# Bank and order changes in a fused attention-and-MLP kernel: two transposing tiles get other PSUM banks, and the instruction lists are reordered

## The chip, the cores and the metric

The kernel runs on one core of a Trainium2 chip. The metric is the device time of one execution in microseconds (us), lower is better. TensorE (PE) multiplies matrices into PSUM, VectorE (DVE), ScalarE (ACT) and GpSimd (POOL) work on tiles, and SyncE (SP) mainly issues transfers (DMAs). The engines run side by side; each takes its own list of instructions in order and waits for the others through semaphores.

## The reference

The output mixes two branches of the same rows x (2048 x 512, bf16) by a gate. Cut to what matters:

```python
x = A_x
g = _sigmoid((x * gate_w).sum(-1, keepdims=True))
# branch a: linear attention, 32 heads of width 16
q, k, v = (x @ wqkv) split into heads
pq, pk = q @ w_phi, k @ w_phi                      # per head
phi = concat(softmax(p), softmax(-p))              # for pq and pk
kv, z = phi_k.T @ v, phi_k.sum(rows)               # per head
o = (phi_q @ kv) / (phi_q @ z + 1e-6)
a = o @ wo
# branch b: MLP
b = relu(x @ w1) @ w2                              # w1: 512 x 1376
return g * a + (1 - g) * b
```

## The kernel before

The rows are 16 tiles of 128, in four chunks of four. Every step of the work is a task with a name; for each engine one list in ORDER (L17 to L63) says in which order its tasks stand, and `emit` (L127) writes them out, with a semaphore wait wherever a task depends on another engine or on a DMA. Nothing is reordered later: what stands first in a list blocks what stands behind it.

Tasks that the prediction speaks of, m a tile, c a chunk, J a job (k0 to k8, q0 to q8, one or two tiles each):

- **Loads** (SP, L276 to L292): xa and xb are the first three tiles of x and the fourth, wva and wvb the halves of the value weights, w1a, w1b and w1c parts of w1; wkT is a transposing load of the key weights, and x1, x2, x3 are transposing loads of the later chunks of x.
- **First chunk of x**: xt{m}a and xt{m}b (L321) turn tile m on TensorE by products with the identity, into two PSUM banks that XB (L317) names; xe{m}0 on ScalarE (L333) and xe{m}1 on VectorE (L335) move them to XT in SBUF. A tile may only be turned once the bank has been emptied of the tile that used it.
- **Values**: v{m} (L369) multiplies a tile with the value weights, for the first four tiles in halves v{m}a and v{m}b, which need wva and wvb; banks 2, 3, 4, 5. ve{m} (ScalarE, L374) moves the result to SBUF.
- **MLP, first half**: h{c}_{k} (L392) and its relu rl{c}_{k} (ScalarE, L410); hr{c} is the remainder with the gate's column (L400), rr{c}, gr{c}, ge{c}, gp{c}, go{c} make the gate's factors, and ht{c} (SP, L421) turns the remainder. Banks 3, 4, 5.
- **Folds**: f1_{j}, f0_{j} (L351) multiply wk or wq with w_phi; fe.. moves them out.
- **Feature jobs**: pr_J (L449) is the projection, ev_J its eviction (ScalarE, L482), mx_J and mn_J maximum and minimum per head (VectorE, L486, L488), t1_J and t2_J the two subtractions (GpSimd, L495), ex_J the exponential (ScalarE, L500), sm_J the sums, rc_J the reciprocals (VectorE), nm_J the scaling (GpSimd, L509 for k, L532 for q); q jobs have ra_J (GpSimd, L528) ahead of nm_J.
- **Key summary**: kv{m} (L516) adds up over all tiles in banks 6 and 7; kn and kz (VectorE, L547, L549) copy it out.
- **Query stage**: tq{m} (SP, L535) turns a tile of query features by DMA, nd{m}_{half} (L559) makes numerators and denominators, rd and o (VectorE, L565, L567) divide, to{m} (SP, L572) turns the result, b{m} (L580) is the second MLP product and a{m} (L586) adds the attention's output product into the same bank, oe{m} (ScalarE, L631) evicts and st{m} stores. b{m} needs the bank that oe{m-3} has emptied. The last tile's b15 and a15 are split in columns (L601, L612), with one part evicted by VectorE (L622).

TensorE's list begins with warm0, a block of idle products (L251), then xt0a to xt2b, the value and MLP products of the first chunk, and the folds. The other engines' lists follow that order of need.

Of the kernel before, what the change touches and what calls it, by code (L numbers as in the profile page):

```python
# [15 lines left out]

ORDER = {  # L17
    "sp": (
        "xa wva xb wvb w1a wphi wkT w1b x1 gw w1c wqT x2 x3 w2a ht0 w2b ht1 wo ht3 tq0 tq1 tq3 tq2 to0 to1 tq4 "
        "tq5 to2 to3 tq6 tq7 to4 ht2 to5 tq9 tq8 to6 to7 tq10 tq11 to8 to9 tq12 tq13 to10 to11 tq14 tq15 to12 "  # L20
        "to13 to14 to15 st15_1 "
    ),
    "pool": (
# [5 lines left out]
    ),  # L29
    "act": (  # L30
# [8 lines left out]
    ),  # L39
    "dve": (  # L40
# [10 lines left out]
    ),  # L51
# [10 lines left out]
    ),  # L62
}  # L63

# [16 lines left out]
class _Graph:  # L81
# [6 lines left out]
    def add(self, name, eng, fn, deps=(), dur=0.1, lat=None, dma=False):  # L88
        assert name not in self.tasks, name
        found = []  # L90
        for d in deps:
            if d is None:
                continue
            t = self.tasks[d]
            if t not in found:
                found.append(t)
        self.tasks[name] = _Task(name, eng, fn, found, dur, self.LAT[eng] if lat is None else lat, dma)
        return name
# [44 lines left out]
def bass_gated_mix__linear_kernel_hedgehog__dense_activation_relu__prompt_kernel(  # L143
# [11 lines left out]
    x2 = A_x.rearrange("b s d -> (b s) d")  # L155
# [25 lines left out]
    with ExitStack() as es:  # L181
# [54 lines left out]
        add = g.add  # L236
# [71 lines left out]
        wbd = [f"wbd{j}" for j in range(ND)]  # L308


        def evict(name, eng, out_, b, deps):
            if eng == "act":
                add(name, eng, lambda q: q.activation(out_, PS[:, b, :], ACT.Copy), deps, dur=0.6)
            else:
                add(name, eng, lambda q: q.tensor_copy(out_, PS[:, b, :]), deps, dur=0.69)

        XB, FB = ((0, 1), (6, 7), (0, 1), (6, 7)), (6, 7, 0, 1)  # L317

        def pe_xt(q, m, n):
            for j in (2 * n, 2 * n + 1):  # L320
                last = q.matmul(PS[:, XB[m][n], (j % 2) * P:(j % 2 + 1) * P], XN[:, m, j * P:(j + 1) * P],  # L321
                                IDN[:, :], start=True, stop=True)
            return last

        for m in range(4):
            for n in range(2):
                add(f"xt{m}{'ab'[n]}", "pe", lambda q, m=m, n=n: pe_xt(q, m, n),
                    ("xa" if m < 3 else "xb", "ident", f"xe{m - 2}{n}" if m > 1 else None), dur=0.11)
            for n, eng in enumerate(("act", "dve")):
                xo = XT[:, 2 * n:2 * n + 2, m * P:(m + 1) * P]  # L330
                xi = PS[:, XB[m][n], 0:2 * P].rearrange("p (j t) -> p j t", j=2)
                if eng == "act":
                    add(f"xe{m}{n}", eng, lambda q, o=xo, i=xi: q.activation(o, i, ACT.Copy), (f"xt{m}a",), dur=0.38)  # L333
                else:
                    add(f"xe{m}{n}", eng, lambda q, o=xo, i=xi: q.tensor_copy(o, i), (f"xt{m}b",), dur=0.42)  # L335
# [13 lines left out]
        def pe_fold(q, s, j, b):  # L349
            for i in range(ND):  # L350
                last = q.matmul(PS[:, b, i * P:(i + 1) * P], WT[:, s * ND + i, j * P:(j + 1) * P], WBD[:, i, :],  # L351
                                start=True, stop=True)
            return last

        for j in range(ND):
            b = FB[j]
            add(f"f1_{j}", "pe", lambda q, j=j, b=b: pe_fold(q, 1, j, b), ("wkT", *wbd, f"xe{3 - j // 2}{j % 2}"), dur=0.24)
            evict(f"fe1_{j}", ("dve", "act")[j % 2], WP[:, 1, j, :], b, (f"f1_{j}",))
        units = []
        for c in range(NC):  # L360
# [6 lines left out]
        def pe_v(q, m, js, b):  # L367
            for j in js:
                last = q.matmul(PS[:, b, :], XT[:, j, m * P:(m + 1) * P], WV[:, j, :],  # L369
                                start=(j == 0), stop=(j == ND - 1))  # L370
            return last

        def evict_v(m, b, deps):
            add(f"ve{m}", "act", lambda q: q.activation(  # L374
                ap(VS, NT * NG * GZ, m * NG * GZ, [[GZ, NG], [1, GV]]), psap(b * 512, [[GV, NG], [1, GV]]), ACT.Copy),
                deps, dur=0.6)

        for m in range(4):
            for n, js in enumerate(((0, 1), (2, 3))):
                add(f"v{m}{'ab'[n]}", "pe", lambda q, m=m, js=js: pe_v(q, m, js, VB[m]),  # L380
                    (f"xe{m}{n}", f"wv{'ab'[n]}", *((f"v{m}a",) if n else ())), dur=0.44)
            evict_v(m, VB[m], (f"v{m}b",))
        freed = {b: (f"ve{m}",) for m, b in enumerate(VB)}
        add("gt", "pe", lambda q: q.matmul(PS[:, 2, 0:ND], GWR[:, :], IDN[:, 0:ND], start=True, stop=True),
# [19 lines left out]
        n = 0  # L404
        for kind, a, k in units:
            b = HB[n % len(HB)]
# [23 lines left out]
        for c in range(NC):  # L430
# [3 lines left out]
                dur=0.2)  # L434
# [3 lines left out]
        for m in range(4, NT):  # L438
            add(f"v{m}", "pe", lambda q, m=m: pe_v(q, m, range(ND), 2), (*xof[m // 4], "wva", "wvb", f"ve{m - 1}" if m > 4 else "gv"),
                dur=0.865)  # L440
# [15 lines left out]
        for jn, (kind, tiles) in enumerate(jobs):  # L456
            w = len(tiles)
            n = kind_n[kind]
# [32 lines left out]
            for tn, M, sg in (("t1", MX, 0), ("t2", MN, 1)):  # L491
                o3 = ap(TS, NTS * 2 * F, ts * 2 * F + sg * GV, [[2 * GV, w * NG], [DH, GH], [1, DH]])
                m3 = ap(M, NSL * 2 * H, sl * 2 * H, [[GH, w * NG], [1, GH], [0, DH]])
                a3, b3 = (pb3, m3) if sg == 0 else (m3, pb3)
# [27 lines left out]
            else:  # L522
# [4 lines left out]
                    dur=0.11 + 0.207 * w)  # L527
# [24 lines left out]
                for m in tiles:  # L552
# [22 lines left out]
                    ab = HB[m % 3]  # L575
# [15 lines left out]
                    if m == NT - 1:  # L591
# [15 lines left out]
                        for h2 in range(2):  # L607
                            b, cs = hb[h2], cols[h2]
# [12 lines left out]
                            else:  # L621
                                add(f"oe{m}_1", "dve", lambda q, m=m, b=b, cs=cs: q.tensor_scalar(  # L622
                                    OSB[:, m % NOS, cs], PS[:, b, 0:cs.stop - cs.start], OMG[:, m:m + 1], None, ALU.mult), need,
                                    dur=0.4)
# [57 lines left out]
```

## Time and profile before

| | |
|---|---|
| median of 3 runs | 150.82 us (150.82 to 150.91) |
| profiled execution | 150.61 us |
| its span in the trace | 148.8 us |
| TensorE busy | 145.4 us, 98% |
| VectorE, GpSimd, ScalarE busy | 110.9, 109.7, 91.8 us |
| chain that ended last, by engine | POOL 46%, PE 42%, issue 5%, DMA 3% |
| TensorE clock granted | full in all 40 slices |

The profile is one execution, taken by the hardware profiler; its time is a little below the median of the runs. Busy time of TensorE is a sum of overlapping bars: a product's bar lasts 379 ns where the next starts 216 ns after it, so pauses are found from starts, not from bars. The chain of waits goes back from the last instruction to whatever released it, again and again. Landing times of DMAs are counted from the start of their issue.

### The profile page before, as it was taken

How to read it: one execution, taken by the hardware profiler on the slowest of the kernel's cores; microseconds unless marked ns; L12 is line 12 of the kernel's file. 1: busy time of each engine (PE TensorE's matmuls, PEld its weight loads, DVE VectorE, ACT ScalarE, POOL GpSimd, SP SyncE). 2: the span in 40 equal slices, each digit the busy share in tenths (PEclk: the TensorE clock that was granted, in tenths of full speed). 3: DMA queues.
4: the chain of work that ended last, by engine and by line, in shares of the span. 5: the costliest groups of instructions: out<-in, count | busy, mean ns of one | idle time of the engine just before them, and what ended most of it. 6: DMA issues, size and time to landing. Idle time of an engine off the chain costs nothing.

```text
span 148.8 us, 2554 instructions
## 1 busy us (share of the span) xinstructions
PE 145.4 (98%) x984; PEld 73.1 (49%) x984; DVE 110.9 (75%) x169; ACT 91.8 (62%) x127; POOL 109.7 (74%) x73
## 2 busy tenths in 40 slices
PE   7999999999999999999999999999999999999994
PEld 2454444445446644455455544454545445445453
DVE  0345799999997769893979979799899966618301
ACT  3367779996795987865988691656545651303051
POOL 4000899999999999999999999999999924510000
PEclk9999999999999999999999999999999999999999
DMA  4999999300200500000000135964737587874543
GB/s 164 289 224 185 261 206 289 109 0 0 66 0 0 154 31 0 0 0 0 4 2 0 35 87 127 108 152 95 181 71 176 151 206 142 162 160 116 127 141 110
DMA packets 45524, 16.11 MB, mean 108 GB/s; under 512 B 39272, under 2 KB 45384, under 8 KB 45512
## 3 DMA queue, kind: packets, MB, share of 16 engines
q1 hardware_dynamic: 43208, 13.89, 42.9%
q10 hardware_dynamic: 2304, 2.06, 4.3%
q8 instruction: 8, 0.13, 0.4%
q14 instruction: 4, 0.03, 0.1%
HBM read 4.41 MB, written 2.10 MB: 44 GB/s over the span
## 4 chain that ended last, share of the span: by engine, by line
POOL 46%; PE 42%; issue 5%; DMA 3%; DVE 1%; SPq 1%; ACT 1%
POOL TS L495 25%; PE PS L580 19%; POOL FT L509 18%; PE PS L586 9%; DMA PHQ<-FT 3%; POOL FT L532 3%; PE PS L559 3%; PE PS L369 2%; PE PS L251 2%; PE PS L449 2%; PE PS L392 2%; PE PS L601 2%; SPq L535 1%; PE PS L321 1%; PE PS L351 1%
## 5 line engine op out<-in xcount | busy, mean ns | idle before, releaser
L495 POOL TENSOR_TENSOR TS<-MN,PB 128x1024 bf16<-128x1024 bf16 (+1 forms) x18 | 31.0, 1733 | 12.9 <-DVE MN L488 12.9
L392 PE MATMUL PS<-XT,W 128*128 128x512 bf16 x160 | 38.4, 379 | 0.0
L502 DVE TENSOR_REDUCE ZB<-FT 128x128 f32<-128x2048 bf16 (+1 forms) x18 | 36.4, 2029 | 1.9 <-ACT FT L500 1.8
L580 PE MATMUL PS<-W,HT 128*128 128x512 bf16 (+1 forms) x165 | 37.8, 379 | 0.0
L500 ACT ACTIVATE FT<-TS 128x2048 bf16<-128x2048 bf16 (+1 forms) x18 | 30.9, 1719 | 4.3 <-POOL TS L495 3.6
L495 POOL TENSOR_TENSOR TS<-PB,MX 128x1024 bf16<-128x1024 bf16 (+1 forms) x18 | 31.1, 1732 | 0.0
L449 PE MATMUL PS<-WP,XT 128*128 128x512 bf16 x128 | 30.1, 379 | 0.0
L509 POOL TENSOR_TENSOR FT<-FT,SC 128x2048 bf16<-128x2048 bf16 (+1 forms) x9 | 29.7, 3308 | 0.0
L631 ACT ACTIVATE OSB<-PS,OMG 128x512 bf16<-128x512 f32 x15 | 10.3, 686 | 24.9 <-PE PS L586 24.8
L410 ACT ACTIVATE HT<-PS 128x512 bf16<-128x512 f32 x40 | 22.6, 596 | 4.7 <-PE PS L392 3.9
L580 PEld LDWEIGHTS PS<-W,HT 128*128 128x128 bf16 (+1 forms) x165 | 15.4, 98 | 17.2 <-ACT OSB L631 0.7
L482 ACT ACTIVATE PB<-PS 128x1024 bf16<-128x1024 f32 (+1 forms) x18 | 16.7, 928 | 10.7 <-PE PS L449 5.7
L392 PEld LDWEIGHTS PS<-XT,W 128*128 128x128 bf16 x160 | 14.7, 98 | 16.4 <-ACT HT L410 0.9
L488 DVE TENSOR_REDUCE MN<-PB 128x64 bf16<-128x1024 bf16 (+1 forms) x18 | 19.4, 1090 | 4.4 <-ACT PB L482 4.3
L486 DVE TENSOR_REDUCE MX<-PB 128x64 bf16<-128x1024 bf16 (+1 forms) x18 | 19.4, 1086 | 3.6 <-ACT PB L482 3.6
L449 PEld LDWEIGHTS PS<-WP,XT 128*128 128x128 bf16 x128 | 12.2, 98 | 14.2 <-ACT PB L482 0.5
L369 PE MATMUL PS<-WV,XT 128*128 128x512 bf16 x64 | 16.4, 379 | 0.1
L532 POOL TENSOR_TENSOR FT<-FT,SR 128x1024 bf16<-128x1024 bf16 (+1 forms) x9 | 15.7, 1740 | 0.6
L586 PE MATMUL PS<-WO,OT 128*128 128x512 bf16 x60 | 14.8, 378 | 0.0
L567 DVE SCALAR_TENSOR_TENSOR OTM<-PS,EG,RD 128x256 bf16<-128x256 f32 x32 | 14.3, 468 | 0.2
L565 DVE RECIPROCAL RD<-PS 128x16 f32<-128x16 f32 x32 | 6.7, 235 | 9.0 <-PE PS L559 9.0
L374 ACT ACTIVATE VS<-PS 128x512 bf16<-128x512 f32 x16 | 9.4, 600 | 2.2 <-PE PS L369 2.2
(54 smaller groups left out, 97.5 us busy)
## 6 DMA issues: line engine op xcount, KB each, us to landing
out_dram<-OSB ACTq DMA_DIRECT2D x15, 128.0 KB, 2.0
W<-in_B_w_dram SPq DMA_DIRECT2D x1, 1280.0 KB, 7.4
W<-in_B_w_dram SPq DMA_DIRECT2D x2, 512.0 KB, 4.9
WV<-in_A_wqkv_dram SPq DMA_DIRECT2D x2, 256.0 KB, 3.7
WO<-in_A_wo_dram SPq DMA_DIRECT2D x1, 512.0 KB, 3.8
FT<-in_A_x_dram SPq DMA_DIRECT2D x1, 384.0 KB, 3.0
W<-in_B_w_dram SPq DMA_DIRECT2D x1, 352.0 KB, 3.6
PHQ<-FT SPq DMA_TRANSPOSE x16, 2.8
```

Of the source, the lines that this page charges most:

```text
L392: last = q.matmul(PS[:, b, :], W1[:, j, k * P:(k + 1) * P], XT[:, j, chunk(c)], start=(j == 0), stop=(j == ND - 1))
L410: add(f"rl{a}_{k}", "act", lambda q, a=a, k=k, b=b: q.activation(HT[:, k, chunk(a)], PS[:, b, :], ACT.Relu), (f"h{a}_{k}",), dur=0.6)
L449: last = q.matmul(PS[:, pj + n, :], XT[:, j, m * P:(m + 1) * P], WP[:, s, j, :], start=(j == 2), stop=(j == 1))
L486: add(f"mx_{J}", "dve", lambda q, sl=sl, w=w, i=pbg: q.tensor_reduce(MX[:, sl, 0:w * H], i, AX.X, ALU.max), (f"ev_{J}", old("t1")), dur=0. ...
L488: add(f"mn_{J}", "dve", lambda q, sl=sl, w=w, i=pbg: q.tensor_reduce(MN[:, sl, 0:w * H], i, AX.X, ALU.min), (f"ev_{J}", old("t2")), dur=0. ...
L495: add(f"{tn}_{J}", "pool", lambda q, o3=o3, a3=a3, b3=b3: q.tensor_tensor(o3, a3, b3, ALU.subtract), (f"{'mx' if sg == 0 else 'mn'}_{J}", ...
L500: add(f"ex_{J}", "act", lambda q, fs=fs, ts=ts, w=w: q.activation(FT[:, fs, 0:w * F], TS[:, ts, 0:w * F], ACT.Exp), (f"t1_{J}", f"t2_{J}", ...
L502: add(f"sm_{J}", "dve", lambda q, fs=fs, sl=sl, w=w: q.tensor_reduce(ZB[:, sl, 0:2 * w * H], FT[:, fs, 0:w * F].rearrange("p (g d) -> p g ...
L509: add(f"nm_{J}", "pool", lambda q, f3=f3, sl=sl, w=w: q.tensor_tensor(f3, f3, SC[:, sl, 0:2 * w * H].unsqueeze(2).to_broadcast([P, 2 * w * ...
L532: add(f"nm_{J}", "pool", lambda q, f3=f3, r3=r3: q.tensor_tensor(f3, f3, r3, ALU.mult), (f"ra_{J}",), dur=0.19 + 0.86 * w)
L580: last = q.matmul(PS[:, ab, :], HT[0:r, k, m * P:(m + 1) * P], W2[0:r, k, :], start=(k == 0), stop=False)
L586: last = q.matmul(PS[:, ab, :], OT[:, m % NOT, t, :], WO[:, t, :], start=False, stop=(t == ND - 1))
```

## The change

Two parts. In the first chunk, tile 2 is turned into banks 4 and 5 instead of 0 and 1, and tile 3 into banks 0 and 1 instead of 6 and 7. The dependencies follow the banks: tile 2's transposes wait for no eviction any more, tile 3's wait for tile 0's, the second half of tile 3's value bank waits for xe21 as well, and the folds wait for the tile that their bank now held. TensorE's list has tile 3 turned before the value product of tile 3, and in part before that of tile 2. The second part is a new order in all five lists from the late key jobs to the end; the number and form of the instructions stay.

```diff
     "sp": (
-        "xa wva xb wvb w1a wphi wkT w1b x1 gw w1c wqT x2 x3 w2a ht0 w2b ht1 wo ht3 tq0 tq1 tq3 tq2 to0 to1 tq4 "
-        "tq5 to2 to3 tq6 tq7 to4 ht2 to5 tq9 tq8 to6 to7 tq10 tq11 to8 to9 tq12 tq13 to10 to11 tq14 tq15 to12 "
+        "xa wva xb wvb w1a wphi wkT w1b x1 gw w1c wqT x2 x3 w2a ht0 w2b ht1 wo ht2 tq0 tq1 tq2 tq3 to0 to1 tq5 "
+        "tq4 to2 to3 tq6 tq7 to4 ht3 to5 tq8 tq9 to6 to7 tq11 tq10 to8 to9 tq12 tq13 to10 tq14 to11 tq15 to12 "
...
     "pool": (
-        "t1_q1 nm_k7 t1_q2 ra_q0 t2_q2 nm_q0 nm_k8 ra_q1 nm_q1 t2_q3 t1_q3 ra_q2 nm_q2 t1_q4 t2_q4 ra_q3 nm_q3 "
+        "t1_q1 nm_k7 t2_q2 ra_q0 t1_q2 nm_q0 ra_q1 nm_k8 nm_q1 t2_q3 t1_q3 ra_q2 t2_q4 nm_q2 t1_q4 t1_q5 ra_q3 "
...
     "act": (
-        "xe00 xe10 xe20 xe30 ve2 ve0 ve1 ve3 fe1_3 rl0_1 fe1_1 rl0_0 ev_k0 rl0_2 ev_k1 ev_k2 ex_k0 rl0_3 rl0_5 "
+        "xe00 xe10 xe20 xe30 ve2 ve1 ve0 ve3 fe1_3 rl0_1 fe1_1 rl0_0 ev_k0 rl0_2 ev_k1 ev_k2 ex_k0 rl0_3 rl0_5 "
...
-        "rl3_5 rl3_9 ev_q5 rl3_8 ge2 ev_q6 ex_q3 oe0 oe1 ex_q4 ev_q7 gp1 oe2 ex_q5 oe3 ev_q8 oe4 ex_q6 oe5 st3 "
+        "rl3_5 rl3_9 ev_q5 ge3 ge2 rl3_8 ev_q6 ex_q3 oe0 oe1 ex_q4 ev_q7 oe2 oe3 ex_q5 ex_q6 oe4 ex_q7 oe5 st0 "
...
     "dve": (
-        "mx_q4 gr3 rc_q1 sm_q2 mn_q5 kn0 kz0 kz1 kn1 mx_q5 rc_q2 rd0_0 rd0_1 o0_0 o0_1 rd1_0 rd1_1 o1_0 o1_1 "
+        "rc_q1 gr3 sm_q2 kn1 kz0 kn0 kz1 mx_q4 mx_q5 rd0_0 o0_0 rd1_0 rd0_1 rc_q2 o0_1 o1_0 rd1_1 o1_1 mn_q5 "
...
     "pe": (
-        "warm0 xt0a xt0b xt1a xt1b xt2a xt2b v0a v2a v1a xt3a v1b v2b xt3b v0b v3a h0_1 v3b h0_0 f1_3 f1_2 f1_0 "
+        "warm0 xt0a xt0b xt1a xt1b xt2a xt2b v0a v1a xt3a v2a xt3b v3a v2b v1b v0b h0_1 v3b h0_0 f1_3 f1_2 f1_0 "
...
-        "kv13 v15 kv14 h3_5 h3_9 b2 h3_8 kv15 b1 nd0_0 nd0_1 pr_q6 nd1_0 nd1_1 b0 nd2_0 pr_q7 a0 nd3_0 nd2_1 a1 "
-        "nd3_1 b3 nd4_1 b4 nd5_0 nd4_0 a2 a3 nd5_1 b5 pr_q8 nd6_0 b6 nd6_1 a4 nd7_0 nd7_1 a5 b7 nd8_0 nd8_1 b8 "
-        "nd9_1 a6 nd9_0 a7 b9 nd10_0 b10 nd11_0 nd10_1 a8 nd11_1 a9 b11 b12 nd12_1 nd12_0 a10 nd13_0 a11 nd14_0 "
-        "nd13_1 nd14_1 b13 nd15_1 nd15_0 b14 a12 a13 a14 b15 a15_0 a15_1 "
+        "kv13 hr3 kv14 h3_9 h3_5 b2 h3_8 kv15 b1 nd0_0 nd1_0 nd0_1 pr_q6 nd1_1 b0 nd2_1 nd2_0 pr_q7 a0 nd3_0 "
+        "nd3_1 a1 b3 b4 nd4_1 nd5_0 nd4_0 a2 a3 nd5_1 b5 pr_q8 nd6_0 b6 nd6_1 nd7_0 a4 nd7_1 a5 b7 nd8_1 nd8_0 "
+        "b8 a6 nd9_0 nd9_1 a7 b9 nd11_0 nd10_0 nd10_1 a8 b10 nd11_1 b11 a9 nd13_0 nd12_0 nd12_1 a10 b12 nd13_1 "
+        "a11 nd14_1 nd14_0 b13 nd15_0 nd15_1 b14 a12 a13 a14 b15 a15_0 a15_1 "
...
-        XB, FB = ((0, 1), (6, 7), (0, 1), (6, 7)), (6, 7, 0, 1)
+        XB, FB = ((0, 1), (6, 7), (4, 5), (0, 1)), (6, 7, 0, 1)
...
-                    ("xa" if m < 3 else "xb", "ident", f"xe{m - 2}{n}" if m > 1 else None), dur=0.11)
+                    ("xa" if m < 3 else "xb", "ident", f"xe0{n}" if m > 2 else None), dur=0.11)
...
-            add(f"f1_{j}", "pe", lambda q, j=j, b=b: pe_fold(q, 1, j, b), ("wkT", *wbd, f"xe{3 - j // 2}{j % 2}"), dur=0.24)
+            add(f"f1_{j}", "pe", lambda q, j=j, b=b: pe_fold(q, 1, j, b), ("wkT", *wbd, f"xe{(1, 3)[j // 2]}{j % 2}"), dur=0.24)
...
-                    (f"xe{m}{n}", f"wv{'ab'[n]}", *((f"v{m}a",) if n else ())), dur=0.44)
+                    (f"xe{m}{n}", f"wv{'ab'[n]}", f"v{m}a" if n else "xe21" if m == 3 else None), dur=0.44)
```

24 rows, old and new, of the table ORDER are left out of this document.

## The prediction

> **What bounds the kernel now.** I read the page first, then the chain of waits piece by piece, then the timeline of the stretches where the chain leaves TensorE or pauses on it, and last the DMA queues of one short window. Names such as v1b or tq2 are those of the order lists.
>
> ```profile
> span 148.8 us, 2554 instructions
> PE 145.4 (98%) x984; PEld 73.1 (49%) x984; DVE 110.9 (75%) x169; ACT 91.8 (62%) x127; POOL 109.7 (74%) x73
> ...
> PE   7999999999999999999999999999999999999994
> ...
> PEclk9999999999999999999999999999999999999999
> ```
>
> TensorE is busy in every slice between the first load and the last product, at the full granted clock. But its bars overlap, so I counted from starts. Four 128x512 products take 0.86 us in the chain, 0.216 each; a pair of the small transposing products (L321) 0.11. Laid end to end at such paces, the work from the first transpose (3.81) to the last product (146.6) leaves only a few pauses. These are they (start, length, instruction, in brackets the idle time before it and what ended it):
>
> ```profile
> 4.57 0.27 PEld L321 LDWEIGHTS PS<-IDN,FT 128*128 128x128 bf16 x4 [0.31 <-ACT XT L333]
> ...
> 5.33 0.11 PEld L369 LDWEIGHTS PS<-WV,XT 128*128 128x128 bf16 x2 [0.38 <-ACT XT L333]
> ...
> 6.51 0.56 PEld L369 LDWEIGHTS PS<-WV,XT 128*128 128x128 bf16 x4 [0.20 <-issue]
> ...
> 12.29 6.21 PE L449 MATMUL PS<-WP,XT 128*128 128x512 bf16 x28
> ...
> 93.66 2.54 PE L580 MATMUL PS<-W,HT 128*128 128x512 bf16 x11
> ...
> 96.35 0.30 PE L559 MATMUL PS<-KVN,PHQ 128*128 128x68 bf16 x4 [0.15 <-DMA PHQ<-FT]
> ```
>
> Matmul starts give the sizes. xt1b starts at 4.16 and xt2a at 4.57 instead of 4.27: 0.30, waiting for ScalarE to empty the bank (xe00). Two small ones, before xt2b and v2a, 0.08 together. xt3a starts at 6.21 and v1b at 6.54 instead of 6.32: 0.22, waiting for the second half of wv (issued 2.17, landing in 4.2, so 6.4). And b0 starts at 93.66 and is through at 96.04, nd2_0 starts at 96.35: 0.32. All others together are below 0.2, apart from some 0.04 at each kv or hr block, which stays. So what a new order can win is bounded by about 0.9 us.
>
> The last pause is a transfer's:
>
> ```profile
> 90.62 1.23 SPq L535
> 91.85 0.04 issue
> 91.90 4.41 DMA PHQ<-FT
> 96.31 0.05 issue
> 96.35 0.30 PE PS L559 x4
> ```
>
> SP issued tq3 at 90.62 and tq2 at 91.90. They landed after 4.8 and 4.4 us, where tq0, tq1 and tq4 took 2.7 to 2.8. The queues from 92 to 94 us, in 40 slices of 50 ns:
>
> ```profile
> DMA  9999999999999995100000039990900000000000
> GB/s 292 282 302 276 302 276 297 282 312 589 282 266 271 271 196 103 26 5 0 0 0 0 0 87 164 215 97 15 5 0 0 0 0 0 0 0 0 0 5 5
> q1 hardware_dynamic: 986, 0.24, 186.6%
> q8 instruction: 1, 0.02, 4.6%
> ```
>
> One instruction packet of 16 KB (4.6% of 16 engines for 2 us is 1.48 us of one engine) starts at 92.47 by the packet records, and the transposes around it nearly stop. SP itself sat 2.59 us on tq2 instead of 1.3, so to0 was issued only at 94.53.
>
> **Head of the kernel, part by part.** Added or removed instructions: none; banks, waits and places change. Laid out with the durations of before:
> - xt2a and xt2b no longer wait for a bank: 4.27 to 4.49. v0a needs xe00 (ScalarE 4.13 to 4.52, TensorE 0.05 later): 4.57, a pause of 0.08. v0a, v1a run to 5.43 (xe10 is done at 4.79).
> - xt3a needs the last x rows (xb, issued 1.67, landing in 3.6: 5.3) and starts at 5.43; v2a to 5.97 (xe20 now ends near 5.1); xt3b to 6.08.
> - v3a is the new wait: xt3a's result is out at 5.43+0.29, xe30 starts 0.04 later, takes 0.38, and TensorE follows 0.05 after: 6.19, a pause of 0.11. Behind it in order stand v2b, v1b, v0b; none of them could start sooner than wvb allows (6.54) in any case.
> - v3a to 6.62; wvb is there, so the old 0.22 pause is gone; v2b, v1b, v0b to 7.92. h0_1 needs w1a (2.65+5.2 = 7.85) and ve2 (v2b out at 7.21, +0.04+0.60+0.05 = 7.90): 7.92 to 7.97. Before it was 8.38, so the lead is 0.41 to 0.46.
> - The folds need wkT, landed near 9.9 (3.71+6.2); they are reached at 10.08 instead of 10.54. Still free.
> - The lead then meets a transfer. The 28 products from 12.29 are two halves of pr_k0, then pr_k1, pr_k2, pr_k3; pr_k2 is the 13th: 12.29+12x0.216 = 14.88. It needs x1, issued 8.48 and landing in 6.0: 14.48. With the lead it is reached at 14.42 to 14.47 and starts 0.05 (as xt0a behind xa) to 0.13 (as v1b behind wvb) after the landing: 14.53 to 14.61. What is left on TensorE is 0.27 to 0.35; I take 0.32, nearer the quicker of these two rows. GpSimd's first subtraction hangs on pr_k0 alone and keeps some 0.43.
>
> From there to the query stage the lists are the same, TensorE shows no pause of size, and GpSimd never idles, so both carry their lead along. **Head: -0.32.**
>
> **Query stage.** Edits where a wait could come up:
> - ra_q1 now stands ahead of nm_k8. It costs nm_k8 0.30 (0.34 less overlap). nm_k8 then ends at 88.31-0.43+0.30 = 88.18; TensorE reaches kv15 at 88.79-0.32 = 88.47. Covered by 0.24. If that cover went, kn, kz and nd0 would be late with it. nm_q1 ends 0.08 sooner than the lead alone gives (the pause between ra_q1 and nm_q1 is filled): 90.6-0.43-0.08 = 90.1.
> - tq2 is now issued ahead of tq3, at 90.1, and nd2 is still behind b0: 96.04-0.32 = 95.72. With the quick landing tq2 is there at 92.9; even with the 4.8 us of the first of the pair in the trace, at 94.9. tq3 with 4.4 is there at 95.8, and nd3_0 is 1.1 us behind nd2. The pause goes either way: **-0.32.**
> - mx_q4, mx_q5 and rc_q2 now stand between kv15 and o0_1 on VectorE. From 88.9: kn and kz 0.95, two maxima 2.24, rd0_0 0.22, o0_0 0.41, rd1_0 and rd0_1 0.3, rc_q2 0.45, o0_1 0.48: 93.95. to0 issues there, to1 1.24 behind; at 2.4 each they land at 96.4 and 97.6. TensorE reaches a0 at 95.72+0.26+0.86 = 96.84 and a1 at 97.96. Cover 0.4 and 0.3: the thinnest of the stage. With SP held on tq3 as it was on tq2 (91.4+2.59 = 94.0), to0 is no later.
> - b7 now has one nd block less between a4 and itself: nd7_1 and a5 are 0.99 long, and a4's drain, eviction (0.69, L631) and return take 0.94. Just covered. b9 and b11 get more room than they had.
> - ht2 and ht3 change places on SP; b8 and b12 want them over 5 us after. Gate steps, stores and the last evictions move on engines with idle time there. The end (a12 to a15_1, then L622 and a store) is as before. All at nothing.
>
> **Sum.** The profiled execution took 150.61 (span 148.8, 1.8 around it): 150.61-0.32-0.32 = 149.97. The runs' median, 150.82, is 0.21 above it: 150.18, given as 150.2.
>
> **Rivals.**
> - *One of the two gains fails* (150.5): x1 lands later or v3a waits longer, or to0/to1 take back 0.3. For it: both covers there are below 0.45 and my landing times come from a single run.
> - *Nothing net* (150.8): both.
> [...]
>
> That trace shows the transposes at 4.8 and 4.4 us around the packet. [...]
>
> **How the numbers follow.** Forecast 0.54 (own range 149.95 to 150.4), one gain fails 0.22, nothing net 0.11, packet on to0 0.13. A measurement of this kernel tells about 0.2%, 0.30 us, from no change. Faster by that: the forecast and more than half of the second case, 0.66. Within: the rest of it and the third, 0.21. Slower: 0.13. The lower end, 149.95, is the head at 0.46 with x1 in time and the small pauses gone; the upper, 150.85, takes in the third case and leaves most of the fourth out.
>
> **What would show it.** xt2a right behind xt1b; a pause near 0.1 before v3a; none before v1b; pr_k2's first load waiting for x1 near 14.5; nd2 without a wait on PHQ; last product near 145.95. Wrong if pr_k2 starts after 14.7, if kv15 waits for L509, or if L586 waits for OT near 97 us.

## The result, and the profile after

The changed kernel takes 152.08 us (median of 8 runs, 151.23 to 153.13) where the kernel before takes 150.79 beside it. The ratio is 1.0082, with a 95% interval of 1.0054 to 1.0109: slower, by about 1.2 us, where 0.6 us less had been forecast. The profiled execution of the changed kernel took 151.68.

The lines of the page that answer to those of before:

```profile
span 149.9 us, 2536 instructions
PE 144.6 (96%) x966; PEld 73.2 (49%) x984; DVE 110.4 (74%) x169; ACT 91.5 (61%) x127; POOL 109.6 (73%) x73
...
PE   7999999999999999999999999999999999996994
...
PE 90%; DMA 5%; ACT 2%; issue 1%; ACTq 1%; DVE 0%
```

The program has as many instructions as before; 18 products lack a record here (966 of 984). One slice of TensorE stands out: the 37th, 135 to 139 us, is busy for six tenths. The same counting as in the prediction, by starts and with the missing products filled in between their neighbours, finds these pauses over 0.07 us after the first transpose: 0.13 before v0a, 0.10 before v3a, 0.10 before v2b, 0.22 before h0_1, 0.08 before pr_k2, and **1.43 before b13**. The pause before nd2 is gone. The last product ends at 147.68 instead of 146.59, 1.09 later; without the pause before b13 it would have ended 0.34 sooner than before.

The chain of waits of the changed kernel goes through that pause (start, length, what):

```profile
130.52 0.70 ACT OSB L631
...
132.09 3.70 DMA out_dram<-OSB
...
135.88 0.70 ACT OSB L631
...
136.62 2.55 PE PS L580 x11
```

And the timeline of ScalarE and TensorE there, in the changed kernel:

```profile
131.24 2.90 ACTq L634 DMA_DIRECT2D out_dram<-OSB  x5
135.88 0.69 ACT L631 ACTIVATE OSB<-PS,OMG 128x512 bf16<-128x512 f32 x1 [4.67 <-DMA out_dram<-OSB]
...
136.62 2.55 PE L580 MATMUL PS<-W,HT 128*128 128x512 bf16 x11 [1.27 <-ACT OSB L631]
```

L631 at 135.88 is oe10, the eviction of tile 10. It did not wait for its product: a10 was through at 131.73. Nor did it wait for ScalarE's queue: the last of five store issues there ended at 134.14. It waited for the landing of a store. The output tile OSB has 8 slots, so oe10 writes the slot of tile 2 and needs the landing of st2. In the changed list five stores (st9, st6, st2, st3, st5) stand in a row behind oe9; st2 was issued at 132.09 and landed 3.70 us later, at 135.79. oe10 starts 0.09 behind that, and b13, which needs the PSUM bank that oe10 empties, stands on TensorE from 135.19 to 136.62, with everything behind it. In the kernel before, st2 went out at 116.59 and landed in 1.7 us, and oe10 waited for its product alone:

```profile
116.59 0.34 ACTq L634 DMA_DIRECT2D out_dram<-OSB  x1
...
134.37 0.69 ACT L631 ACTIVATE OSB<-PS,OMG 128x512 bf16<-128x512 f32 x1 [5.01 <-PE PS L586]
```

In the head, the loads set the pace. These are weight loads of TensorE in the changed kernel:

```profile
6.82 0.98 PEld L369 LDWEIGHTS PS<-WV,XT 128*128 128x128 bf16 x6 [0.43 <-DMA WV<-in_A_wqkv_dram]
8.32 0.56 PEld L392 LDWEIGHTS PS<-XT,W 128*128 128x128 bf16 x4 [0.52 <-ACT VS L374]
```

The first is v2b, held for the second half of wv, which landed at 6.78 here and at 6.4 in the profile of the kernel before. The second is h0_1. The bracket names ScalarE (ve2), but ve2 had ended at 8.07; w1a landed at 8.21 (2.65 and 5.6 us), against 7.84 in the kernel before. pr_k2 started at 14.93 behind the landing of x1 at 14.80, not at the 14.53 to 14.61 of the prediction, and not before the 14.88 of the kernel before.

### The profile page after: what moved, and what is told of

It is laid out like the page before. It is cut to its first block, busy times and chain, and to the rows that moved or that the text cites. A ratio compares the mean times of both kernels' runs of the same rounds, so it can differ in the third digit from the quotient of the medians.

```text
span 149.9 us, 2536 instructions
## 1 busy us (share of the span) xinstructions
PE 144.6 (96%) x966; PEld 73.2 (49%) x984; DVE 110.4 (74%) x169; ACT 91.5 (61%) x127; POOL 109.6 (73%) x73
## 4 chain that ended last, share of the span: by engine, by line
PE 90%; DMA 5%; ACT 2%; issue 1%; ACTq 1%; DVE 0%
PE PS L392 23%; PE PS L580 22%; PE PS L449 18%; PE PS L369 9%; PE PS L586 7%; PE PS L516 3%; DMA out_dram<-OSB 2%; PE PS L559 2%; DMA FT<-in_A_x_dram 2%; PE PS L601 2%; PE PS L400 1%; PE PS L351 1%; ACT OSB L631 1%; PE PS L321 1%; PE PS L612 1%
## 5 line engine op out<-in xcount | busy, mean ns | idle before, releaser
L580 PE MATMUL PS<-W,HT 128*128 128x512 bf16 (+1 forms) x158 | 36.9, 379 | 1.6 <-ACT OSB L631 1.3
L631 ACT ACTIVATE OSB<-PS,OMG 128x512 bf16<-128x512 f32 x15 | 10.2, 686 | 27.3 <-PE PS L586 19.4
L392 PEld LDWEIGHTS PS<-XT,W 128*128 128x128 bf16 x160 | 14.7, 98 | 16.8 <-ACT HT L410 0.6
```

What stands on the lines that cost most here:

```text
L392: last = q.matmul(PS[:, b, :], W1[:, j, k * P:(k + 1) * P], XT[:, j, chunk(c)], start=(j == 0), stop=(j == ND - 1))
L580: last = q.matmul(PS[:, ab, :], HT[0:r, k, m * P:(m + 1) * P], W2[0:r, k, :], start=(k == 0), stop=False)
```

## The experiments

**Theory S:** st2's late landing holds oe10, oe10 holds b13, and that is the loss. **Rivals:** the crowd of stores and transposes near 133 us costs by itself (C); ScalarE is held by issuing five stores (Q); the head made it slower (H). For the gains that did not come: the loads take the head's lead (L), and both gains were traits of one execution (V). Times are medians, with the ratio to the kernel before on the same chip and its 95% interval; the medians of before were 150.82, 150.56 and 150.73 in the three batches of experiments. The ratio is estimated from all executions and is not the quotient of the two medians, which differs from it by up to 0.13% here.

| run | median us | ratio | interval | pause before b13 |
|---|---|---|---|---|
| changed kernel | 152.08 | 1.0082 | 1.0054 to 1.0109 | 1.43 |
| e1_slots15 | 150.97 | 1.0000 | 0.9979 to 1.0021 | below 0.1 |
| e2_head_only | 150.53 | 0.9994 | 0.9972 to 1.0017 | below 0.1 |
| e3_query_only | 152.25 | 1.0090 | 1.0058 to 1.0123 | 1.58 |
| e4_tq_swap | 150.45 | 0.9979 | 0.9956 to 1.0002 | below 0.1 |
| e5_st2_first | 150.91 | 1.0028 | 1.0003 to 1.0052 | below 0.1 |
| e6_stores_late | 150.95 | 1.0020 | 0.9999 to 1.0041 | below 0.1 |
| e7_head_v3b | 150.87 | 1.0014 | 0.9994 to 1.0034 | below 0.1 |
| e8_head_v3b_swap | 150.60 | 0.9996 | 0.9971 to 1.0022 | below 0.1 |
| e9_slots15_v3b | 150.98 | 1.0006 | 0.9985 to 1.0027 | below 0.1 |

**The slot's wait taken away.** The changed kernel with one number altered:

```diff
-    NPH, NOM, NOT, NOS = 6, 3, 4, 8
+    NPH, NOM, NOT, NOS = 6, 3, 4, 15
```

> The changed kernel with 15 output slots instead of 8, all orders kept, so that oe10 needs no landing of st2. Theory S (oe10 waits for the landing of st2, b13 for oe10): the pause of 1.43 us before b13 falls below 0.2, the time falls from 152.1 to 150.5 to 150.9. Rival C (the late products are slowed by the crowd of stores and transposes itself, whichever slot is used): the pause moves to another block near 135 us and the time stays above 151.5.

```profile
134.29 0.69 ACT L631 ACTIVATE OSB<-PS,OMG 128x512 bf16<-128x512 f32 x1 [2.94 <-PE PS L580]
...
135.34 2.54 PE L580 MATMUL PS<-W,HT 128*128 128x512 bf16 x11
```

In this run's timeline oe10 starts at 134.29, as soon as the five stores are issued (131.39 and 2.86), and b13 follows the work before it without a pause. st2 itself landed as late as ever, at 135.56. The time fell by 0.8% of before, to 0.07 above the range expected. Theory S holds; rival C does not explain the loss, since no other block took over the pause. What is left is the kernel before's time, not 0.64 less.

**The head alone.** The kernel before with the graph's lines of the diff, TensorE's first list line and ScalarE's ve2, ve1, ve0 of the changed kernel.

> The kernel before with the bank change and the new head order alone. If the head gains as predicted and nothing behind it eats the gain: 150.79-0.32, 150.4 to 150.6, the last product 0.3 earlier. Rival L (the loads land when they land and the head ends on w1a or x1): within 0.15 of before. Rival H (the head is what made the change slower): above 151.3.

0.9994 with an interval of 0.9972 to 1.0017: no change that can be told. The median lies in the range of the gain, and a gain of 0.32 (0.9979) is inside the interval too, so the time alone does not decide. The profile shows where the lead went: w1a landed at 8.22, TensorE paused 0.42 before h0_1, and x1 landed at 14.99, which cost another 0.27 before pr_k2 (15.12). H falls.

**The query stage alone.** The changed kernel with banks, dependencies and head lists of before.

> The changed kernel with the old head and old banks, so the new query stage alone. Theory S puts the whole loss here: 152.0 to 152.5, with the pause of 1 to 1.6 us before b13. Rival H: near 150.8.

The whole loss is there: 1.0090, st2 issued 133.46 and landed 137.30, oe10 at 137.38, a pause of 1.58. (The profiled execution, 153.3, lost another 1.4 at the start: wvb landed at 7.75 in it.)

**tq2 first.**

```diff
-... wo ht3 tq0 tq1 tq3 tq2 to0 to1 tq4 ...
+... wo ht3 tq0 tq1 tq2 tq3 to0 to1 tq4 ...
```

> The kernel before with tq2 issued ahead of tq3 and nothing else. If the pause of 0.32 us before nd2_0 hangs on which of the two is issued first: the pause goes and the time is 150.3 to 150.6. If the packet of instructions holds whichever transpose nd2 needs: the pause stays, 150.8.

No pause before nd2_0 in its profile: tq2 landed at 95.14 and nd2_0 started at 95.94. The median lies in the range expected, the interval just reaches 1: a gain is likely, not shown.

**The same stores in another order.** The changed kernel, with

```diff
-... oe9 st9 st6 st2 st3 st5 oe10 ...
+... oe9 st2 st9 st6 st3 st5 oe10 ...
```

> The changed kernel, 8 slots, with st2 as the first of the five stores behind oe9 instead of the third; the same five stores still stand ahead of oe10. Theory S (it is st2's landing that holds oe10): st2 is issued near 131.3 and lands near 134 to 135, oe10 starts by then, the pause before b13 falls from 1.4 to 1.6 us to below 0.5, the time from 152.1 to 150.7 to 151.3. Rival Q (ScalarE is held by issuing five stores, whichever comes first): oe10 stays near 135.9 and the time above 151.7.

```profile
130.94 2.84 ACTq L634 DMA_DIRECT2D out_dram<-OSB  x5
133.88 0.69 ACT L631 ACTIVATE OSB<-PS,OMG 128x512 bf16<-128x512 f32 x1 [2.26 <-DMA out_dram<-OSB]
...
135.60 2.54 PE L580 MATMUL PS<-W,HT 128*128 128x512 bf16 x11
```

As the first of the five, st2 landed at 133.02, 2.1 us behind its issue instead of 3.7, and oe10 started at 133.88, right behind the fifth issue. b13 did not pause. oe10 ended at 134.57, 1.0 us ahead of b13's start. So the five issues, 2.84 us of ScalarE's queue, are covered, and the landing was the wait: Q falls. The ratio is still 1.0028, with an interval just above 1.

**Five late stores in the kernel before.**

```diff
-... oe5 st3 ge3 gp2 gp3 st2 ex_q7 oe6 st1 st6 oe7 st5 ex_q8 st0 oe8 st8 oe9 oe10 oe11 st11 st4 ...
+... oe5 ge3 gp2 gp3 ex_q7 oe6 st1 oe7 ex_q8 st0 oe8 oe9 st9 st6 st2 st3 st5 oe10 oe11 st8 st11 st4 ...
```

> The kernel before with st9, st6, st2, st3 and st5 issued in a row behind oe9, as in the changed kernel. There a9 stands four blocks ahead of a10, here a9 is 5.7 us ahead of oe10's data. Theory S: st2 lands near 133.5 and oe10 is ready for it at 134.3, so no pause before b13 beyond 0.2 and 150.6 to 151.0: the stores cost only where the evictions stand close. Rival C (five late stores cost by themselves): above 151.5.

st2 was issued at 129.97 and landed at 132.68; a10's data for oe10 came at 134.24. No pause before b13, and 150.95: the wait for the slot is covered where oe9 stands 5.9 us ahead of oe10, and not where, as in the changed order, a9 is only three small blocks (nd13_0, nd12_0, nd12_1) ahead of a10. The row of stores is not free here either:

```profile
135.27 0.43 PEld L559 LDWEIGHTS PS<-KVN,PHQ 128*128 128x128 bf16 x12 [0.57 <-DMA PHQ<-FT]
```

This is nd14_0, waiting for tq14. Issued at 130.58, in the middle of the row of stores, tq14 landed after 4.65 us, where it took 2.79 in the kernel before, and TensorE paused 0.24 by starts. So rival C is right in small, in this profile: the crowd costs something, but not the 1.2 us.

**More cover for w1a.** The head alone, and the head with tq2 first, both with

```diff
-... v2b v1b v0b h0_1 v3b h0_0 ...
+... v2b v1b v0b v3b h0_1 h0_0 ...
```

> The kernel before with the new banks and head, and v3b ahead of h0_1 as well, so that 0.43 us of work stands before the first user of w1a. Theory L (w1a's landing at 7.7 to 8.4 takes the head's lead): the pause of 0.22 to 0.42 before h0_1 falls below 0.1 and pr_k2 starts near 14.6 to 14.8 unless x1 holds it; 150.3 to 150.6. Rival: the lead is taken by x1 or wkT all the same, pr_k2 at 14.9 or later and no change from the head alone.

> The same as the run with v3b ahead of h0_1, and tq2 issued ahead of tq3. If both pauses go independently: 150.0 to 150.4, below each alone. If the lead of the head is lost to loads: as the swap alone, 150.4 to 150.5.

The pause before h0_1 went in both (w1a at 8.23 and 7.95, h0_1 at 8.89 and 8.56, with no pause). The times did not follow: 1.0014 and 0.9996, neither to be told from before, and both medians, 150.87 and 150.60, lie above the ranges expected. pr_k2 started at 15.01 and 14.63. In the first of these TensorE's opening products ran at half pace until 5.2 (last section), which the new banks can't help.

**Both kernels profiled again, and the changed one with both mends** (15 slots, and v3b ahead of h0_1).

> The kernel before, unchanged, looked at once more. Theory V (both gains of the prediction were read from traits of a single execution): the pause before nd2_0 is below 0.15 or absent, or w1a lands 0.2 or more away from the first look's 7.84. Rival F (they are fixed): nd2_0 waits 0.25 to 0.4 again and w1a lands within 0.1 of 7.84.

> The same kernel a third time, with the same expectations: under theory V at least one of the two looks shows no pause at nd2_0, and the landings of w1a spread over 0.3 us or more; under rival F all three looks agree.

The kernel before, profiled three times: w1a landed at 7.84, 8.04 and 7.91; the pause before nd2_0 was 0.32 and then below 0.1 twice. tq2 landed late in all three (96.31, 95.88, 96.31), but in the second run it landed earlier, and in the third TensorE came later (nd2_0 started at 96.40). In the two runs of the head without the swap, also with tq3 first, it landed at 94.7 and cost nothing. Theory V holds for this pause. For w1a these three alone spread by 0.2 only; over thirteen of the fourteen profiles of all kernels it is 7.65 to 8.46, and 9.11 in the other.

Theory V holds for the head as well. The two pauses that the new head takes away were 0.30 (before xt2a) and 0.22 (before v1b) in the first profile of the kernel before. With the same head they were 0.17 and none in r1_before, 0.05 and none in r2_before, and 0.05 and 0.01 in e6_stores_late: TensorE opened at half pace there (last section), so it came later to the points at which it had waited.

> The changed kernel looked at once more. Theory S: oe10 again starts right behind st2's landing, and b13 pauses 1.0 to 2.0 us; no other pause behind the head exceeds 0.3. If the pause were a trait of one execution, it is below 0.3 here.

```profile
136.38 1.30 ACT L631 ACTIVATE OSB<-PS,OMG 128x512 bf16<-128x512 f32 x2 [4.45 <-DMA out_dram<-OSB]
...
137.12 2.12 PE L580 MATMUL PS<-W,HT 128*128 128x512 bf16 x9 [1.05 <-ACT OSB L631]
```

The same wait: st2 landed at 136.29, oe10 started at 136.38, and by starts b13 paused 1.21. With 1.43 and 1.21 in the two profiles of the changed kernel, and 1.58 in that of its query stage, the pause is no trait of one execution.

> The changed kernel with 15 slots and with v3b ahead of h0_1. If the store was the whole loss and the head's lead is kept from w1a: 0.2 to 0.5 below before, ratio 0.997 to 0.999. If the lead is lost to the next landing or to jitter: no difference from before, ratio 0.999 to 1.002.

1.0006, 0.9985 to 1.0027: no difference. No version tried here beats the kernel before beyond its interval; tq2 first alone comes nearest.

## Why the prediction was wrong

**The step that failed** is the one that put "gate steps, stores and the last evictions" on "engines with idle time there", "all at nothing". ScalarE did have the time. But a store is a transfer with a landing, and its landing gives back an output slot: st2 was moved from 116.59 to 132.09, oe10 needs its landing, and b13 needs oe10. The cover was the time between st2's landing and oe10's need: some 16 us before (118.28 to 134.37), none after (135.79, with a10 through at 131.73). Shown: taking away the wait for the slot, or moving st2 two places ahead, each ends the pause and brings the time back to within 0.3% of before. None of the prediction's cases named this wait; the slower one, the packet on to0, had another place and another transfer.

**The instruction packet and to0** (the slower case, at 0.13: the packet delays to0, and a0 waits for it): not what happened. Where the packet would fall in the new order was the author's estimate, from TensorE's place in its list. In the first profiles of the two kernels it did come at one place, with 620 and 619 of the 984 weight loads started, at 92.47 and 91.73. But with the query order of before it came at 89.7 and 90.0 in the profiles of the head alone and of the head with v3b, so that it keeps to a place was not shown. In the changed kernel tq2 landed at 94.54 and tq3 at 95.41, to0 was issued at 94.09 and landed at 96.38, before a0 needed it at 97.12.

**Query stage, the other steps.** tq2 first took the wait out of nd2 as worked out, kv15 did not wait for nm_k8, and b7 did not pause. The term of 0.32 was mis-sized as a typical gain: it was there in one of three profiles of the kernel before. Its late transfers come back, the pause hangs on a few tenths.

**The head.** The waits moved as worked out: xt2a followed xt1b at once, v3a paused 0.10, and the 0.22 before v1b went. The size was wrong, for two reasons. The pauses to be saved were those of one opening, as the profiles of the kernel before show. And the term rested on w1a landing at 7.85 and h0_1 starting at 7.92 to 7.97; h0_1 started at 8.35 behind a landing at 8.21. In the first profile of the changed kernel, in e2_head_only and in e1_slots15, with w1a at 8.2 to 8.4, h0_1 paused 0.22, 0.42 and 0.23, and pr_k2 stood at 14.93, 15.12 and 15.02 against a predicted 14.53 to 14.61; a start after 14.7 was the prediction's own sign of being wrong. In the second profile of the changed kernel w1a came at 8.46 and h0_1 did not wait, because TensorE, at half pace, reached it only at 9.08. Over all profiles no lead is to be seen: pr_k2 started at 14.63 to 15.59 in eight with the new head, at 14.79 to 15.25 in five with the old one, and at 16.23 in the one whose wvb landed at 7.75. Whether the new head itself makes w1a land later is open: 7.65 to 8.46 in eight profiles with it, 7.74 to 8.04 in five without it and 9.11 in a sixth. The load is issued at 2.64 or 2.65 in all fourteen, before the first transpose, so the scatter of the loads is the nearer guess. The two gains together, 0.64, should have been left once the wait for the store was gone. Measured was 1.0000, with an interval that ends at 0.9979, 0.32 us.

## What to carry to other kernels

When an order moves a store, price it like a load: find who needs the buffer back, and lay the time from the new issue to that need against the landing, not against the issuing engine's idle time. st2's landing took 1.7 us alone in the kernel before, and 3.7 as the third of five in a row beside transposes in the changed one. And before a pause of a few tenths goes into a sum as a gain, profile the kernel more than once: here pauses of 0.2 to 0.4 us came and went between executions, while the store's wait came back, 1.21 to 1.58 us, in every profile of the changed query stage with 8 slots and st2 third.

## What the runs showed of the hardware

TensorE's opening products ran at half pace, 427 ns from start to start of a 128x512 product where it was 216 later, until a moment that differed from execution to execution. The first transposes (L321; duration min/median/max) in the first profile of the kernel before and in its third:

```profile
L321 PE MATMUL PS<-IDN,FT x8: 219/219/230, 3.8 to 4.2; 128*128 128x128 bf16 x8
```

```profile
L321 PE MATMUL PS<-IDN,FT x12: 287/314/314, 4.0 to 5.2; 128*128 128x128 bf16 x12
```

By starts it is 56 and 107 ns for a 128x128 product. The change of pace came before 3.9 us in the first profile of either kernel, and near 5.7 and 6.2 in later ones of the one and the other. The page gives the granted clock as full in every slice, but the trace's records of the clock begin only with the faster pace: at 3.62 and 3.88 us in the first profiles of the kernel before and the changed one, and at 5.72 in r2_before. Nothing is recorded ahead of that, and the page counts it as full. In the slow openings of the old head the pause before xt2a shrinks from 0.30 to between 0.05 and 0.17, since the turning itself takes longer (107 ns a product instead of 56), so the bank change has less to win there. What sets the moment was not shown: the nine traces that have such records begin them between 3.43 and 5.81, 2.4 us apart, and the records at full clock last 146.77 us in four of them and 143.36 in five.

How long tq1 and tq2 took to land went with where a 16 KB instruction packet fell. In twelve profiles the packet came at 91.4 to 92.8, while tq2 was under way, and tq2 took 3.85 to 4.6 us to land. In the two others, of the head alone and of the head with v3b, it came at 89.7 and 90.0, before tq3 and tq2 were issued (90.65 and 91.92 in the one). There tq2 took 2.8, and tq1, which now had the packet beside it, took 4.3 and 4.7 instead of 2.8. That the packet is what slows the transposes is an inference from this; no run moved it alone.
